# A sliding-window attention and SiLU feed-forward kernel: how the first two attention units are finished, and the order of the work

## The chip, the cores and the metric

The kernel runs on one core of a Trainium2 chip. The core has TensorE (PE, with its weight loads shown apart as PEld), VectorE (DVE), ScalarE (ACT), GpSimd (POOL) and SyncE (SP). In this kernel POOL issues all loads and SP all stores. The metric is the device time in microseconds of one execution.

## The reference

Inputs are `q`, `k`, `v` of shape (8 batches, 8 heads, 576 positions, 64), `w_in` (512 x 2048) and `w_out` (2048 x 512), all in 32-bit floats.

```python
scores = (q @ k.T) / sqrt(64)            # for each batch and head
scores = where(0 <= i - j < 64, scores, -1e9)
attn   = softmax(scores)
x      = (attn @ v), heads side by side   # 4608 tokens x 512
h      = x @ w_in
out    = (h * sigmoid(h)) @ w_out
```

A position sees itself and the 63 before it, so a block of 64 queries needs the keys and values of two blocks of 64.

## The kernel before, in words

**Tiling.** The 72 blocks of 64 positions (9 for each batch) are taken four at a time: 18 units `u`, each 256 tokens wide and all 8 heads deep. The feed-forward part takes 9 tiles `j` of 512 tokens, so tile `j` needs units `2j` and `2j+1`.

**A unit.** Loads bring queries and keys into `nat`. VectorE turns them in 32 x 32 blocks (L322, L332, L335). For the first five units `shift_k` (L311) copies the keys of the block before into place. The score matmuls (L397, L374) fill four PSUM banks, and ScalarE takes the exponential (L403) into `es`. For units 0 and 1 the mask enters the scores as a bias: a matmul of `ident` with `window` (L388). Later units multiply by `mask` on VectorE (L406). The value matmuls (L437, L425) have `es` as the stationary operand and `vv` as the moving one. `vv` has a column of ones beside the 64 values, so each output row carries its own sum in column 64. VectorE inverts 8 sums per row (L442) and multiplies (L445) into `oxs`. For units in `BACK` (0, 1, 2, 3, 5), four PE transposes (L461) and a copy (L464) bring the result into `bridge`, which holds `x` transposed. For the others a DMA transpose on SP does it (L455). Units 0 and 1 do this in two halves `hf`, each with its own PSUM banks.

**Values.** `load_v(b, t)` fills the 128 rows of `vv` at `t` with blocks `t-1` and `t`. For odd `t` it is a load (L345), for even `t` the two halves are copied from the neighbours by `shift_v` (L365, L367). `add_v` takes the list of loads and of copies; `v0` and `v1` hold them for batches 0 and 1.

**Feed-forward.** Tile 0 has its own path. `add_first` issues, for each 128 columns `ft` of `w_in`, four matmuls (L470 from `first_layer`) into one bank and a SiLU (L478). Six `ft` are done first for tokens 0 to 255, then for 256 to 511 (`NF0 = 6`, so that the first half can begin when unit 0 is done), the other ten at full width. `add_plain_second` then runs 64 matmuls of 512 columns, in the order of `f`, and needs `w_out` piece by piece. Later tiles use a form with seven products in place of eight for the second layer, and tiles 6 to 8 for the first layer too (L509).

**What sets the order.** The class `Plan` simulates the engines with costs (`us`), latencies and a model of the DMA queue, and picks at each step, on each free engine, the waiting operation with the lowest `first` (its rank by class). The order it finds is then written out as the program of each engine, so an instruction that waits holds all behind it on its engine. `GO` gives for each unit from 2 on how many feed-forward matmuls must have been issued before its scores may start. `SEQ` is the order of POOL's first loads: `a` to `e` are keys and queries of units 0 to 4, `v` and `y` the next group of value loads of batch 0 and 1, `w` and `o` pieces of `w_in` and `w_out`, `i` the constants. `pick_halves` writes a run of feed-forward matmuls next to value matmuls as pairs of 64 columns each when the run is short against `HALVES`. `UP = 4` puts the scores of unit 1 into banks 4 to 7. A filler matmul on `blank` (L974) keeps PE at work until the first feed-forward matmul.

**Constants.** GpSimd makes `window` and `ident` (L247 to L255) behind the third group of loads. ScalarE copies half of `window` into `window0` (L259), and VectorE makes `mask` (L262, L263). VectorE clears `kt` (L270), the three `vv` (L266, L267) and part of `k2` (L958) at the start.

Of the kernel before, what the change touches and what calls it, by code (L numbers as in the profile page):

```python
# [8 lines left out]
FP32 = mybir.dt.float32  # L9
# [8 lines left out]
class Plan:  # L18
# [7 lines left out]
    def __init__(self, pools, rank):  # L26
        self.rank, self.pools = rank, pools
        self.queues = {}
        self.banks = [[] for _ in range(8)]
        self.count = 0  # L30
        self.halves_cost, self.halves_end, self.halves_not = 0, 0, ()
        self.now = 0.0

    def add(self, cls, us, fn, deps=(), lat=0.2, gate=None, dma=None, pool=None, table=None, rank=None, late=0.0):
        op = dict(us=us, first=self.rank[cls] if rank is None else rank, fn=fn,
                  deps=[d for d in deps if d is not None], lat=lat, gate=gate, dma=dma,
                  pool=pool, table=table, late=late, halve=False, seen=None, n=self.count, until=[], untils=None, bank=None)
        self.count += 1
        self.queues.setdefault(cls, []).append(op)
        return op  # L40
# [99 lines left out]
def kernel(ctx, tc, q, k, v, w_in, w_out, out):  # L140
# [29 lines left out]
    EX = 2  # L170
    LATE = [0, 0, 1, 3, 4, 4, 4, 4]
    scale = 1.0 / float(D) ** 0.5
# [8 lines left out]
    zero = keep.tile([128, 4], FP32, name="zero")  # L181
    spare = keep.tile([128, 4], FP32, name="spare")
# [48 lines left out]
    def pair(op):  # L231
# [3 lines left out]
        {"quad": [(0, 1, 2, 3)], "upper": [(4, 5, 6, 7)], "pp": [(0, 1), (2, 3)], "at": [(0,), (2,)],  # L235
         "mp": [(i,) for i in range(4, 8)], "idle": [(i,) for i in range(4, 8)] + [(0,), (2,)], "all": [(i,) for i in range(8)]},
        rank=dict(one=-9, first=-9, late=5, dma=-1, st=-2, kshift=-16.3, xo=-58.5, turn=11.8, shift=13.7,
                  s=-33.1, exp=-9.0, mask=4.1, pv=27.6, inverse=-8.9, norm=-15.8, ot=-17.4, bridge=-27.4,
                  silu=9.0, moe=99, warm=200, sum=7.1, xsum=-35.5, asum=34.0, plus=-19.9, stage=2.1, wsum=-0.6, piece=-31.8, out=-3.6, prime=-8,
                  turn2=-1.4, turn1=-37.9, shift0=-7.7, shift0b=8.7, shift1=25.9, inverse0=6.3, norm0=1.4, bridge0=16.5,),  # L240
# [5 lines left out]
    def const_ident(_):  # L246
        nc.gpsimd.memset(ident, 0.0)  # L247
        nc.gpsimd.affine_select(out=ident, in_=ident, compare_op=ALU.not_equal, fill=1.0,
                                base=0, channel_multiplier=1, pattern=[[-1, 128]])

    def const_window(_):
        nc.gpsimd.memset(window, 0.0)
        nc.gpsimd.affine_select(out=window, in_=window, compare_op=ALU.is_ge, fill=-32768.0,
                                base=-1, channel_multiplier=1, pattern=[[-1, 64]])
        nc.gpsimd.affine_select(out=window, in_=window, compare_op=ALU.is_ge, fill=-32768.0,  # L255
                                base=64, channel_multiplier=-1, pattern=[[1, 64]])

    def const_window0(_):
        nc.scalar.copy(out=window0[64:128], in_=window[64:128])  # L259

    def const_mask(_):
        nc.vector.tensor_scalar(mask[:, 0], window, 1.0 / 32768.0, 1.0, op0=ALU.mult, op1=ALU.add)  # L262
        nc.vector.tensor_copy(out=mask[:, 1:], in_=mask[:, 0:1].to_broadcast([128, 15, 64]))  # L263
# [9 lines left out]
    c_k = [p.add("one", {"DVE": 0.1}, lambda _, i=i: clear_k(i)) for i in range(2)]  # L273
    c_vv = [p.add("one", {"DVE": 0.4}, lambda _, i=i: clear_vv(i)) for i in range(NVB)]
    c_low = p.add("one", {"DVE": 0.1}, lambda _: nc.vector.memset(window0, -32768.0))
# [8 lines left out]

    def add_consts():
        c_window = p.add("dma", {"POOL": 0.8}, const_window)
        c_ident = p.add("dma", {"POOL": 0.6}, const_ident)
        c_window0 = p.add("prime", {"ACT": 0.25}, const_window0, [c_window, c_low], rank=-9)
        return c_ident, c_window0, p.add("late", {"DVE": 0.8}, const_mask, [c_window])
# [150 lines left out]

    def inverse(op, r, hf):
        nc.vector.reciprocal(out=rcs[r], in_=at_pv(op, hf)[:, :, :, D])  # L442
# [29 lines left out]
    def first_layer(op, bk, j, ft, c, lo, hi):  # L472
        v0 = 4 * j % NBR
        expert_mm(op, bank(bk)[:, lo:hi], w_in_sb[:, c, ft * 128:(ft + 1) * 128],
                  bridge[:, v0 + lo // 128:v0 + hi // 128, c], start=(c == 0), stop=(c == NDC - 1))

    def silu(bk, ft, lo, hi):
        nc.scalar.activation(out=gts[0][:, ft, lo:hi], in_=bank(bk)[:, lo:hi], func=ACTF.Silu)  # L478
# [87 lines left out]
    exps0 = []  # L566
# [31 lines left out]
    def add_v(b, ts, shifts):  # L598
# [4 lines left out]
        for low, a, z in shifts:  # L603
            n = len(range(a, z, 2))
            sh = p.add("shift", {"DVE": 0.1 + 0.2 * n, "ACT": 0.2 + 0.38 * n} if b < 2 else {"DVE": 0.1 + 0.22 * n}, lambda e, low=low, a=a, z=z: shift_v(e, b, low, a, z),
                       [d for t in range(a, z, 2) for d in v_done[b, t - 1 if low else t + 1]],
                       rank=p.rank[("shift0" if a < 4 else "shift0b") if b == 0 else "shift1"] if b < 2 else None)
            for t in range(a, z, 2):
                v_done.setdefault((b, t), []).append(sh)
# [27 lines left out]
    def add_scores_blocks(u):  # L637
        if u < 2:
            bi = p.add("bias", {"PE": 0.95}, lambda _: bias(u), [c_window0, c_ident] + (s_new[0] + kb_done[1][:1] if u else []), pool="upper" if u and UP else "quad", rank=-6)
# [49 lines left out]
    def add_units(u, ready):  # L689
# [8 lines left out]
        for hf in range(2):  # L698
            n = n_unit[0]
# [44 lines left out]
    def add_first(j, pool):  # L744
        jobs = [(ft, 0, TT) for ft in range(NFT)]
        if j == 0:
            jobs = [(ft, 0, HT) for ft in range(NF0)] + [(ft, HT, TT) for ft in range(NF0)] + jobs[NF0:]
        si, bks = {}, {}
        for n, c in [(n, c) for n in range(len(jobs)) for c in range(NDC)]:
            ft, lo, hi = jobs[n]  # L750
            have = [d for i in range((j * TT + lo) // 256, (j * TT + hi) // 256) for d in o_done[i]]
# [3 lines left out]
            op["fn"] = lambda _, op=op, bk=bk, ft=ft, c=c, lo=lo, hi=hi: first_layer(op, bk, j, ft, c, lo, hi)  # L755
            moe.append((op, 1, n == 0 and c == 0, j))
            if c == NDC - 1:
                sl = p.add("silu", {"ACT": 0.18 + (hi - lo) * 0.00082}, lambda _, bk=bk, ft=ft, lo=lo, hi=hi: silu(bk, ft, lo, hi),
                           [op] + g_users[0].get(ft, []) + (exps0 if j == 0 else []), table="silu")
                bk["until"] = [sl]  # L760
                for h in range(lo // HT, hi // HT):
                    si.setdefault((ft, h), []).append(sl)
# [197 lines left out]
    v1 = list(v0)  # L960
    for z in SEQ:
# [4 lines left out]
        elif z == "i":  # L966
            c_ident, c_window0, c_mask = add_consts()
# [11 lines left out]
    c_mask["deps"].append(s_new[0][0])  # L979
# [75 lines left out]
```

## Time and profile before

| what | value |
|---|---|
| median of 3 runs | 281.4 us (281.08 to 281.74) |
| the profiled execution | 282.42 us |
| its span, first to last instruction | 280.6 us |
| mean granted TensorE clock | 0.994 |
| PE busy | 271.8 us (97%) |
| VectorE, ScalarE, GpSimd busy | 203.7, 175.8, 109.3 us |

Times in the rows count from the start of the span. A row of the timeline merges neighbouring instructions of one kind: start, length, engine, line, operation, output and inputs, count, and in brackets the idle time of the engine before it and what ended that. A row of the chain of waits has start, length, and engine with line. A row of the windows has the stretch, its length, then the busy time of PE, PEld, VectorE, ScalarE and GpSimd with instruction counts, the granted clock, and the load of the DMA engines. A row of groups has the shapes and the count, then busy time and mean duration in ns of one, then the idle time before.

### The profile page before, as it was taken

How to read it: one execution, taken by the hardware profiler on the slowest of the kernel's cores; microseconds unless marked ns; L12 is line 12 of the kernel's file. 1: busy time of each engine (PE TensorE's matmuls, PEld its weight loads, DVE VectorE, ACT ScalarE, POOL GpSimd, SP SyncE). 2: the span in 40 equal slices, each digit the busy share in tenths (PEclk: the TensorE clock that was granted, in tenths of full speed). 3: DMA queues.
4: the chain of work that ended last, by engine and by line, in shares of the span. 5: the costliest groups of instructions: out<-in, count | busy, mean ns of one | idle time of the engine just before them, and what ended most of it. 6: DMA issues, size and time to landing. Idle time of an engine off the chain costs nothing.

```text
span 280.6 us, 8735 instructions
## 1 busy us (share of the span) xinstructions
PE 271.8 (97%) x3704; PEld 197.2 (70%) x3704; DVE 203.7 (73%) x380; ACT 175.8 (63%) x272; POOL 109.3 (39%) x163
## 2 busy tenths in 40 slices
PE   8799999999999999899999999999999999999995
PEld 4367445446876488566885488647888888888884
DVE  4682458999868599789698568947587867868641
ACT  2768884976568683857637675665556664565631
POOL 8976776649787599584680000000000000000000
PEclk9979999999999999999999999999999999999999
DMA  9999999999999999999999602540013001101303
GB/s 85 172 197 187 186 185 185 220 220 143 123 217 164 126 146 153 152 177 139 134 165 189 71 2 77 97 96 0 4 37 112 3 32 67 57 0 40 112 20 132
DMA packets 105863, 32.42 MB, mean 116 GB/s; under 512 B 90464, under 2 KB 104800, under 8 KB 105824
## 3 DMA queue, kind: packets, MB, share of 16 engines
q0 software_dynamic: 82336, 19.02, 84.4%
q1 hardware_dynamic: 23488, 12.85, 22.6%
q8 instruction: 29, 0.48, 0.8%
q14 instruction: 10, 0.08, 0.1%
HBM read 38.01 MB, written 9.44 MB: 169 GB/s over the span
## 4 chain that ended last, share of the span: by engine, by line
PE 83%; DMA 8%; issue 3%; DVE 3%; POOL 2%; ACT 1%; DVEq 0%; POOLq 0%; ACTq 0%
PE mp L470 57%; PE la L509 8%; PE la L470 6%; PE mp L509 5%; DMA vv<-in_v_dram 3%; PE at L374 2%; DMA nat<-in_k_dram 2%; PE at L425 2%; DMA nat<-in_q_dram 2%; PE at L437 1%; POOL vv L345 1%; PE at L461 1%; PE mp L974 1%; POOL nat L316 1%; DVE eo L406 1%
## 5 line engine op out<-in xcount | busy, mean ns | idle before, releaser
L470 PE MATMUL mp<-bridge,w_in_sb 128*128 128x512 bf16 (+3 forms) x521 | 86.7, 367 | 0.2 <-ACT gt L478 0.2
L478 ACT ACTIVATE gt<-mp 128x512 bf16<-128x512 f32 (+1 forms) x102 | 56.6, 573 | 22.0 <-PE mp L470 21.2
L470 PEld LDWEIGHTS <-w_in_sb 128*128 128x128 bf16 (+1 forms) x521 | 41.4, 103 | 38.0 <-issue 0.8
L470 PEld LDWEIGHTS <-gs 128*128 128x128 bf16 x512 | 49.4, 98 | 6.0
L403 ACT ACTIVATE eo<-at 128x1024 bf16<-128x1024 f32 x34 | 34.0, 1027 | 14.0 <-PE at L374 12.7
L470 PEld LDWEIGHTS <-gt 128*128 128x128 bf16 (+1 forms) x422 | 34.1, 102 | 9.5 <-issue 0.4
L470 PE MATMUL mp<-ws,gs 128*128 128x256 bf16 x320 | 40.3, 273 | 0.0
L470 PE MATMUL mp<-w_out_sb,gt 128*128 128x256 bf16 (+3 forms) x278 | 38.6, 310 | 0.0
L345 POOL DMA_DIRECT2D vv<-in_v_dram x38 | 33.6, 898 | 3.0 <-DMA w_out_sb<-in_moe_w_out_dram 1.3
L293 POOL DMA_DIRECT2D nat<-in_q_dram x40 | 24.0, 608 | 17.8 <-DMA vv<-in_v_dram 10.0
L406 DVE TENSOR_TENSOR eo<-eo,mask 128x1024 bf16<-128x1024 bf16 x32 | 21.6, 681 | 6.9 <-ACT eo L403 6.7
L293 POOL DMA_DIRECT2D nat<-in_k_dram x40 | 24.2, 617 | 6.1 <-DMA nat<-in_k_dram 3.0
L909 ACT COPY ot<-mp 128x512 f32<-128x512 f32 (+1 forms) x28 | 15.8, 563 | 15.5 <-PE mp L470 14.4
L520 ACT ACTIVATE eo<-vv 128x512 bf16<-128x512 f32 (+1 forms) x18 | 13.9, 773 | 16.2 <-DVE vv L800 16.2
L445 DVE TENSOR_TENSOR eo<-at,rc 128x512 bf16<-128x512 f32 x36 | 22.9, 674 | 0.2
L533 DVE TENSOR_TENSOR gs<-gt 128x1024 bf16<-128x1024 bf16 x24 | 16.3, 686 | 8.5 <-ACT gt L478 8.5
L912 DVE TENSOR_TENSOR ot<-mp,ot 128x512 f32<-128x512 f32 (+1 forms) x21 | 13.8, 658 | 5.7 <-PE mp L470 4.6
L800 DVE TENSOR_TENSOR vv<-mp,vv 128x512 f32<-128x512 f32 x15 | 10.3, 689 | 7.1 <-PE mp L509 7.1
L509 PEld LDWEIGHTS <-w_in_sb 128*128 128x128 bf16 x144 | 14.1, 98 | 1.6
L800 DVE TENSOR_TENSOR vv<-la,vv 128x512 f32<-128x512 f32 x21 | 13.8, 683 | 2.0 <-PE la L509 1.7
L470 PE MATMUL mp<-w_out_sb,gs 128*128 128x256 bf16 x112 | 14.0, 273 | 0.0
L470 PE MATMUL mp<-ws,gt 128*128 128x256 bf16 (+1 forms) x128 | 11.8, 273 | 0.2 <-DVE ot L912 0.2
(121 smaller groups left out, 384.7 us busy)
## 6 DMA issues: line engine op xcount, KB each, us to landing
out_dram<-ot SPq DMA_DIRECT2D x32, 256.0 KB, 3.3
vv<-in_v_dram POOLq DMA_DIRECT2D x38, 128.0 KB, 6.6
nat<-in_k_dram POOLq DMA_DIRECT2D x40, 72.0 KB, 5.8
nat<-in_q_dram POOLq DMA_DIRECT2D x40, 72.0 KB, 5.5
w_in_sb<-in_moe_w_in_dram POOLq DMA_DIRECT2D x8, 256.0 KB, 8.4
w_out_sb<-in_moe_w_out_dram POOLq DMA_DIRECT2D x8, 256.0 KB, 8.1
out_dram<-ot SPq DMA_DIRECT2D x8, 128.0 KB, 1.8
nat<-in_k_dram POOLq DMA_DIRECT2D x3, 256.0 KB, 6.2
```

The lines of the kernel that those rows point to most:

```text
L293: nc.gpsimd.dma_start(out=nats[i].bitcast(BF16)[32 * r:32 * r + 32].rearrange("s (g y) -> s g y", y=128), in_=(q, k)[kk][b, h].rearrange(" ...
L345: nc.gpsimd.dma_start(out=vv[b % NVB][:, t, :, 0:D], in_=v[b, :, 64 * t - 64:64 * t + 64].rearrange("h s d -> s h d"),)
L403: nc.scalar.activation(out=dst, in_=src, func=ACTF.Exp, scale=scale)
L406: nc.vector.tensor_mul(es[w], es[w], mask)
L445: nc.vector.tensor_mul(oxs[o].rearrange("p x c (r d) -> p x (c r) d", r=2), at_pv(op, hf)[:, :, :, 0:D], rcs[r].unsqueeze(3).to_broadcast( ...
L470: nc.tensor.matmul(o[cols], lhsT=w[:, cols], rhs=x, **kw)
L478: nc.scalar.activation(out=gts[0][:, ft, lo:hi], in_=bank(bk)[:, lo:hi], func=ACTF.Silu)
L509: nc.tensor.matmul(bank(bk)[:, HT * f:HT * f + HT], lhsT=w[:, c, 128 * (2 * u + f):128 * (2 * u + f) + 128], rhs=rhs, start=first and f == ...
L520: nc.scalar.activation(out=gt_of(j)[:, f0:f0 + 2, lo:hi], in_=src, func=ACTF.Silu)
L533: (nc.vector.tensor_sub if i else nc.vector.tensor_add)(sums[i][:, f0:f1], x[:, f0:f1], y[:, f0:f1])
L800: d[k] = p.add("plus", {"DVE": 0.69}, lambda _: nc.vector.tensor_add(o, halves(bk), o), [op] + deps)
L909: return p.add("piece", {"ACT": 0.18 + 0.0008 * n}, lambda e: copies[e](out=flat(o), in_=bank(bk)[:, 0:n]), [end] + deps)
```

## The change

- Units 0 and 1 (`TURNED`): the value matmuls swap their operands, so `vv` is stationary (64 columns, without the column of ones) and `es` is moving, and the result lies transposed, as `bridge` wants it. The sums come from matmuls of a 128 x 64 tile of ones with `es` into a second bank, where each sum stands in all 64 rows of its head. VectorE inverts a whole bank of 128 x 512 (`rts`) and multiplies bank by bank into `bridge`. The transposes and copies to `bridge` of these two units go.
- The constants are made on VectorE by `consts` at the start. `window0` and the bias need no other engine. The clearing of `vv[2]` and `kt` and the full `mask` wait for unit 1 (`o_done[1]`).
- Tile 0's half-width jobs take two `ft` in one bank, eight `ft` are done so (`NF0 = 8`), and one SiLU of 128 x 512 serves two `ft`.
- The order: `SEQ`, `GO`, all ranks, `HALVES` and `WHOLE` are new, `NUDGE` moves two single operations, unit 1's scores use banks 0 to 3 (`UP = 0`), and the first value copies of batch 0 are split.

```diff
-    GO = [8, 64, 16, 220, 288, 68, 393, 172, 480, 200, 569, 588, 248, 746, 404, 496]
+    GO = [72, 9, 161, 245, 196, 313, 402, 0, 275, 371, 593, 638, 8, 752, 37, 780]
-    NF0 = 6
-    HALVES = 30
-    WHOLE = []
+    NF0 = 8
+    HALVES = 70
+    WHOLE = [0, 1, 2, 3, 4, 6, 7, 11, 13, 14, 17, 23, 24, 26, 27, 30, 31, 33]
-    SEQ = "a v b i v w w w o w w w y w o w c d o o v y o o e o o y".split()
+    TURNED = (0, 1)
+    SEQ = "a b v w v w w w o w w w w o v c d o o y o y o o o e y".split()
-    UP = 4
+    UP = 0
+    NUDGE = {21: -11.3, 341: 39.7}
...
-    def const_ident(_):
-        nc.gpsimd.memset(ident, 0.0)
-        nc.gpsimd.affine_select(out=ident, in_=ident, compare_op=ALU.not_equal, fill=1.0,
...
+    def consts(_):
+        t = bridge[:, 12:14].rearrange("p v c i -> p (v c i)").bitcast(FP32)
+        col, row, low = t[:, 0:128], t[:, 128:160], t[:, 160:192].bitcast(BF16)
+        nc.vector.memset(col[:, 0:1], 0.0)
+        for w in (1, 2, 4, 8, 16, 32, 64):
+            nc.vector.tensor_scalar_add(col[:, w:2 * w], col[:, 0:w], float(w))
+        nc.vector.transpose(out=row, in_=col[:, 0:32])
+        for r in range(1, 4):
+            nc.vector.tensor_scalar_add(row[32 * r:32 * r + 32, 0:1], row[32 * r:32 * r + 32, 0:1], 32.0 * r)
+        nc.vector.tensor_scalar(col, col, row[:, 0:1], None, op0=ALU.subtract)
+        nc.vector.tensor_scalar(ident, col, 0.0, None, op0=ALU.is_equal)
+        nc.vector.tensor_scalar(low, col[:, 0:64], 0.0, None, op0=ALU.is_lt)
+        nc.vector.scalar_tensor_tensor(out=mask[:, 0], in0=col[:, 0:64], scalar=-64.0, in1=low, op0=ALU.is_ge, op1=ALU.mult)
+        nc.vector.tensor_scalar(window, mask[:, 0], 32768.0, -32768.0, op0=ALU.mult, op1=ALU.add)
+        nc.vector.memset(window0[0:64], -32768.0)
+        nc.vector.tensor_copy(out=window0[64:128], in_=window[64:128])
...
+    def sums_turned(op, u, z):
+        o = bank_at(op["bank"][1]).rearrange("p (c a i) -> p c a i", c=H // 2, a=2)
+        e = es[(2 * u + z) % NE].rearrange("p (a c x) i -> p x a c i", a=2, c=H // 2)
+        for a in range(2):
+            for x in range(2):
+                nc.tensor.matmul(o[64 * x:64 * x + 64, :, a], lhsT=ones, rhs=e[:, x, a], start=(a == 0), stop=(a == 1))
+
+    def values_turned(op, u, z):
+        o = bank_at(op["bank"][0]).rearrange("p (c a i) -> p c a i", c=H // 2, a=2)
+        for a in range(2):
+            b, t = divmod(4 * u + 2 * z + a, NB)
+            for c in range(H // 2):
+                for x in range(2):
+                    nc.tensor.matmul(
+                        o[64 * x:64 * x + 64, c, a], lhsT=vv[b % NVB][:, t, 2 * c + x, 0:D],
+                        rhs=es[(2 * u + z) % NE][:, 8 * a + 2 * c + x], start=(a == 0 and c == 0), stop=(a == 1 and c == H // 2 - 1))
+
+    def inverse_turned(op, z):
+        nc.vector.reciprocal(out=rts[z], in_=bank_at(op["bank"][1]))
+
+    def normal_turned(op, u, z):
+        nc.vector.tensor_mul(bridge_out(u, z).rearrange("p c i -> p (c i)"), bank_at(op["bank"][0]), rts[z])
...
+            if u in TURNED:
+                two = [2 * hf, 2 * hf + 1]
+                sm = p.add("pv", {"PE": 0.3}, None, ready[hf] + [c_ones], pool="pp" if u else "pu", rank=-5.6)
...
-            jobs = [(ft, 0, HT) for ft in range(NF0)] + [(ft, HT, TT) for ft in range(NF0)] + jobs[NF0:]
+            jobs = [(ft, lo, lo + HT) for lo in (0, HT) for ft in range(0, NF0, 2)] + jobs[NF0:]
...
+    v0[0] = ((1, 3), ((0, 0, 2), (1, 2, 4), (0, 2, 4)))
...
-    c_mask["deps"].append(s_new[0][0])
+    for c in [c_mask] + c_vv[2:] + c_k:
+        c["deps"].extend(o_done[1])
+    for sh in shifts_late:
+        sh["deps"].append(exps0[1])
```

More of the change, by code (lines that the diff above doesn't have):

```diff
@@ L181 @@
     zero = keep.tile([128, 4], FP32, name="zero")
+    ones = keep.tile([128, 64], BF16, name="ones")
+    rts = [keep.tile([128, 512], FP32, name=f"rt{i}") for i in range(2)]
     spare = keep.tile([128, 4], FP32, name="spare")
@@ L272 @@
     c_blank = p.add("one", {"DVE": 0.15}, lambda _: nc.vector.memset(blank.bitcast(FP32), 0.0))
[L273 to L275 removed]
+    c_const = p.add("one", {"DVE": 2.0}, consts)
+    c_vv = [p.add("one" if i < 2 else "clear", {"DVE": 0.5}, lambda _, i=i: clear_vv(i)) for i in range(NVB)]
+    c_k = [p.add("clear", {"DVE": 0.1}, lambda _, i=i: clear_k(i)) for i in range(2)]
+    c_mask = p.add("late", {"DVE": 0.7}, const_mask, [c_const])
+    c_ones = p.add("one", {"DVE": 0.1}, lambda _: nc.vector.memset(ones, 1.0))
     c_zero = p.add("one", {"DVE": 0.1}, lambda _: nc.vector.memset(zero, 0.0))
@@ L283, in load_wide @@
         )
[L285 to L289, printed above, removed]
     def load_rows(i, b, h, kk):
```

79 lines of the change are left out of this document (44 added, 35 removed).

## The prediction

> **What bounds the kernel now.** I read the page first, then PE's busy time by stretches of the span.
>
> ```profile
> span 280.6 us, 8735 instructions
> PE 271.8 (97%) x3704; PEld 197.2 (70%) x3704; DVE 203.7 (73%) x380; ACT 175.8 (63%) x272; POOL 109.3 (39%) x163
> ...
> 10.70:15.20 4.50, 2.16 (x85) 1.19 (x82) 3.98 (x8) 3.29 (x5) 4.38 (x7) 1.00 1.87 180
> 15.20:19.30 4.10, 4.10 (x74) 2.61 (x66) 3.39 (x8) 3.55 (x6) 3.19 (x4) 0.58 1.38 198
> 19.30:33.70 14.40, 14.40 (x114) 9.07 (x111) 4.98 (x11) 11.38 (x24) 9.91 (x13) 1.00 1.69 186
> 33.70:52.00 18.30, 18.30 (x369) 10.00 (x368) 13.61 (x27) 12.77 (x20) 12.94 (x18) 1.00 1.60 190
> ...
> 191.50:276.70 85.20, 85.20 (x783) 76.37 (x781) 60.80 (x99) 47.06 (x80) 0.00 (x0) 1.00 0.14 46
> ```
>
> PE is full from 19.3 us to the end. So a change pays if it starts the feed-forward part earlier, shortens PE's work, or removes one of PE's few waits. The start is read from the timeline and from the chain of waits.
>
> ```profile
> 5.65 0.71 DVE L322 STREAM_TRANSPOSE kt<-nat 128x512 f32<-128x512 f32 x1 [2.08 <-DMA nat<-in_k_dram]
> 7.09 0.72 DVE L322 STREAM_TRANSPOSE qt<-nat 128x512 f32<-128x512 f32 x1 [0.21 <-DMA nat<-in_q_dram]
> 8.05 0.29 DVE L365 COPY vv<-vv 64x512 bf16<-64x512 bf16 x1 [0.23 <-DMA vv<-in_v_dram]
> 9.61 0.33 DVE L365 COPY vv<-vv 64x512 bf16<-64x512 bf16 x1 [1.27 <-DMA vv<-in_v_dram]
> 11.06 0.71 DVE L322 STREAM_TRANSPOSE gs<-nat 128x512 f32<-128x512 f32 x1 [1.12 <-DMA nat<-in_k_dram]
> 14.58 0.21 DVE L442 RECIPROCAL rc<-at 128x8 f32<-128x8 f32 x1
> 19.29 1.25 PE L470 MATMUL mp<-bridge,w_in_sb 128*64 128x256 bf16 x20
> 21.59 12.29 PE L470 MATMUL mp<-bridge,w_in_sb 128*128 128x256 bf16 x72
> 33.71 0.59 PE L470 MATMUL mp<-w_out_sb,gt 128*128 128x512 bf16 x2
> ```
>
> The loads land one after the other, 1.45 us apart for keys and queries and 2.5 us for two of values. Unit 0 is ready to be inverted at 12.3 us but waits until 14.58, because VectorE is turning unit 1 (11.06 to 14.55). Then come inverse, multiply, transpose and copy for two halves, and the first feed-forward matmul starts at 19.29. From there tile 0's first layer runs without a hole until 33.7.
>
> **The new start, loads.** Two rows of the DMA view give issue to landing of the fourth and the eighth piece of `w_in`:
>
> ```profile
> 12.72 0.83 POOL L351 DMA_DIRECT2D w_in_sb<-in_moe_w_in_dram  x1
> w_in_sb<-in_moe_w_in_dram POOLq DMA_DIRECT2D x1, 256.0 KB, 8.1
> ...
> 19.78 0.77 POOL L351 DMA_DIRECT2D w_in_sb<-in_moe_w_in_dram  x1 [0.58 <-DMA w_out_sb<-in_moe_w_out_dram]
> w_in_sb<-in_moe_w_in_dram POOLq DMA_DIRECT2D x1, 256.0 KB, 9.5
> ```
>
> They land at 12.72 + 8.1 = 20.8 and 19.78 + 9.5 = 29.3. Between them lie four pieces of weights and two of values, 8.5 us, so about 1.35 a piece of weights if a piece of values takes 0.75 to 1.25. In the new order the fourth piece has one piece of `w_out` less ahead of it: 20.8 - 1.35 = 19.5. The eighth has one piece of `w_out` and two of values less: about 26.5. Counting back from 19.5, pieces 3, 2 and 1 land near 18.1, 16.8 and 13.3. Unit 1's keys and queries now follow unit 0's (8.5 and 10.0), and the first values come at 12.5 instead of 9.6. POOL loses its constants, but they cost no landing: the load behind them, issued at 8.04, still queued behind others for 5 us.
>
> **The new start, VectorE.** These rows price it:
>
> ```profile
> L445 DVE TENSOR_TENSOR eo<-at,rc 128x512 bf16<-128x512 f32 x36 | 22.9, 674 | 0.2
> L912 DVE TENSOR_TENSOR ot<-mp,ot 128x512 f32<-128x512 f32 x19 | 13.0, 682 | 4.9 <-PE mp L470 3.8 <-ACT eo L403 0.7
> L912 DVE TENSOR_TENSOR ot<-mp,ot 128x256 f32<-128x256 f32 x2 | 0.8, 424 | 0.8 <-PE mp L470 0.8
> L442 DVE RECIPROCAL rc<-at 128x8 f32<-128x8 f32 x36 | 6.7, 197 | 3.4 <-PE at L425 2.3 <-PE at L437 0.2
> L262 DVE TENSOR_SCALAR mask<-window 128x64 bf16<-128x64 bf16 x1 | 0.4, 380 | 0.0
> L276 DVE MEMSET zero<- 128x4 f32 x1 | 0.1, 62 | 0.0
> ```
>
> - Constants: 17 small instructions, between 0.06 and 0.38 each by the last two rows, 1.0 to 6.5 us. I take 0.2 each, 3.4 us, since both kinds are among them. With two clearings of `vv` and the rest, VectorE is free at about 6.0 instead of 5.65. The cover is the wait for the first keys. At the upper bound the first turn slips to 9.0, and the value loads, which wait for the clearing, slip by 1.1 us with all behind them: 1.1 us lost.
> - Reciprocal of a whole bank: not in this trace. The 256- and 512-wide rows give 1.0 ns an element and 0.17 fixed. Lower bound 0.17 + 512 ns = 0.68. If what the 128x8 inverse has above the fixed part (0.207 - 0.168 for 8) were all by element, 5 ns each, it is 2.7 us. I take 0.7: the bank's shape and path are those of L445 and L912, and the small inverse reads single columns 65 apart, which explains its rest as well. The Trainium skill (VectorE: DVE Perf Modes, "First, the fixed hardware budget") says that reciprocal runs iterated divide steps with a repeat count of 8; taken as eight cycles an element, my estimate from that page would be 4.4 us, and no run here has shown it.
> - The sum: from 8.5 us on VectorE has two turns (1.4), two of the key copies (1.1), four reciprocals (2.8), four multiplies (2.7), six value copies (2.3): 10.3 us, so unit 1 is in `bridge` at 18.8 or later, and unit 0 about 14.5. Values of unit 1 land near 16.2, then copy, value matmul and two multiplies end by 19 as well.
>
> **The new start, PE.** Clearing, mask and transposes are off its path. What PE adds (sums and turned values, 20 matmuls in place of 16 for each half) is bounded by the value matmuls that go, 0.5 us a half from below, and 0.9 with four 256-wide ones at 0.11 each. It lies in holes, because tile 0's first half now waits for `w_in`. The 32 matmuls of 256 columns per half (0.109 each: 64 of them in 7.0) come in four groups of 0.87 us with pieces 1.35 apart, so the first half ends 0.87 after the fourth piece: 20.4. The granted clock speaks for a little more:
>
> ```profile
> 12.00:13.00 1.00, 0.26 (x16) 0.14 (x10) 0.97 (x3) 0.97 (x2) 1.00 (x3) 1.00 2.33 175
> 13.00:14.00 1.00, 0.11 (x2) 0.10 (x2) 0.94 (x3) 0.98 (x2) 1.00 (x2) 1.00 1.46 186
> 16.00:17.00 1.00, 1.00 (x4) 0.49 (x4) 0.94 (x3) 1.00 (x3) 0.93 (x2) 0.50 1.45 201
> 18.00:19.00 1.00, 1.00 (x27) 0.80 (x26) 0.51 (x2) 0.90 (x2) 0.49 (x1) 0.50 1.40 199
> ```
>
> PE's idle time before 15 us brought the clock to half from 16 to 19. Now it hits feed-forward work: 0 to 0.6 us more, and I take 0.3. So the second half starts at 20.7 (unit 1 is in by then), runs 3.5 us, and eight full `ft` follow at 4 x 0.214 = 0.855 each, 6.85 us, with the eighth piece there in time: 31.05 against 33.7. **Gain 2.65 us** (3.3 at best).
>
> **After 31 us.** The bytes loaded until 49 us are the same, and the last pieces of `w_out` come earlier, so tile 0's second layer should hold its 18.3 us less what moved. PE's other waits are these:
>
> ```profile
> 55.67 4.41 PEld L470 LDWEIGHTS <-w_in_sb 128*128 128x128 bf16 x21 [0.37 <-issue]
> 117.97 0.54 PE L425 MATMUL at<-vv,eo 128*64 128x65 bf16 x22 [1.20 <-issue]
> 144.27 1.94 PE L470 MATMUL mp<-ws,gt 128*64 128x256 bf16 x32 [0.24 <-DVE ot L912]
> ...
> 42.68 0.51 PE at L437 x32
> 63.39 0.63 PE at L437 x32
> ```
>
> With two smaller ones they sum to 2.1 us. The gates of late units move by up to 34 matmuls (unit 13 from 588 to 638, of which 8 are tile 0's longer list), which can shift each wait either way. Bounds: 2.1 gained, or the 2.65 given back where loads, which do not move, set the time. I take 0.5 gained, since the later gates put scores where the loads are surely there. `HALVES` and `WHOLE` choose at which value matmuls PE changes its tiling; the last two rows show 0.12 us for one side. At most five units can gain or lose that: 0.6 either way, taken as 0.
>
> **Sum.** 282.42 for the profiled execution (280.6 span and 1.8 around it) less 2.65 and 0.5 is 279.27. That execution was 1.0 above the median of 281.4, so the median becomes **278.2**.
>
> **Rivals.**
> 1. *More*: the clock holds (0.3), all waits go (1.6 beyond mine) and halving pays 0.6: near 275.7. For it: every wait is short and has its own cause. Against it: a fixed order cannot remove all.
> 2. *Given back*: the gain turns into waits of units 7 to 13. For it: the chain of waits leaves PE between 122 and 147 us.
>
> ```profile
> 125.00 9.72 DMA vv<-in_v_dram
> 135.01 5.56 DMA nat<-in_q_dram
> ```
>
> There loads, not PE, set the time of unit 13, though PE idled only 0.4 us. If its place in PE's order stays, PE waits the 2.65 us instead: 281.4. Against it: its gate moves back.
> 3. *Slower by a misplaced unit*: unit 2's scores may now follow the 72nd matmul of tile 0, at about 25.9 us. Its queries land near 31.3 (26.5 for the eighth piece, then a piece of `w_out` 1.35, half a piece of values 0.6, keys and queries 2.9) and are ready at 32.2. If the planner's DMA model runs ahead and puts them there, PE, which takes its program in order, stands for 6.3 us: 278.2 + 6.3 = 284.5. It is slower than before from a wait of 3.2 us. Against it: before, the gate was 8 and the scores still came after 90 matmuls, at 34.2, once loaded.
> 4. *Slow reciprocals*: at 2.7 us each VectorE's sum grows by 8.0, unit 1 is in at 26.8, the first layer ends at 37.2, 3.5 later than before: 284.4 with the 0.5 kept. Slower from about 1.9 us each, where unit 1 comes in after 23.8. By the skill's figure it would be about 291.
> 5. *It does not do what it says*: the constants at their upper bound leave 1.1 us less, 279.3, within the forecast's own range.
>
> **How the numbers follow.** Forecast and rival 5, 276.8 to 280.5: 0.60. More: 0.12. Given back: 0.11, of which 0.07 within 0.2%. Misplaced: 0.10. Slow reciprocals: 0.05. Unnamed: 0.02. About 0.2%, 0.6 us, is what a measurement here can tell from no change. Faster 0.76, same 0.07, slower 0.17. The range 275.2 to 282.0 leaves the two slow rivals out; the likeliest case's own is 276.8 to 280.5.
>
> **What would show it.** Right: feed-forward starts near 14.5 to 15.5 us with holes until 20 to 21, each ended by a piece of `w_in`; the first 512-wide matmul on `w_out` near 31; whole-bank reciprocals of 0.7 us; no ACT or PE work for transposes of units 0 and 1. Wrong: reciprocals of over 1.9 us, VectorE still busy with constants after 7 us, a wait of PE's scores of unit 2, or waits after 50 us that sum to more than 4 us.

## The result, and the profile after

The changed kernel takes 289.51 us in the median (289.47 to 290.75, four runs), the kernel before 281.24 in the same runs (279.96 to 281.74): a ratio of 1.031 with a 95% interval of [1.027, 1.036]. Forecast were 278.2 us and a range of 275.2 to 282.0, so the sign was wrong. The profiled execution took 290.75 us, 8.3 more than that of before.

The page of the changed kernel and then its stretches come first, with the columns as in the prediction. The stretches end at unit 0's scores, at the first feed-forward matmul, at the start of tile 0's second layer, at tile 1, at tile 6 and at the end.

```profile
span 289.0 us, 8803 instructions
PE 273.7 (95%) x3739; PEld 198.5 (69%) x3739; DVE 219.9 (76%) x400; ACT 171.3 (59%) x258; POOL 108.6 (38%) x158
```

```profile
0.00:11.44 11.44, 8.14 (x29) 3.67 (x30) 9.36 (x32) 2.52 (x3) 10.41 (x17) 0.85 1.32 118
11.44:22.86 11.42, 7.03 (x195) 4.17 (x194) 10.49 (x11) 7.82 (x10) 6.67 (x10) 1.00 1.58 192
22.86:43.67 20.81, 17.22 (x132) 10.93 (x132) 11.95 (x15) 9.24 (x16) 14.89 (x20) 0.84 1.64 187
43.67:62.01 18.34, 17.94 (x280) 9.10 (x279) 14.36 (x31) 10.84 (x16) 13.14 (x20) 1.00 1.65 172
62.01:200.68 138.67, 138.47 (x2331) 94.84 (x2331) 112.40 (x216) 94.60 (x136) 63.48 (x94) 1.00 1.24 126
200.68:285.60 84.92, 84.87 (x778) 75.83 (x775) 61.35 (x99) 45.90 (x79) 0.00 (x0) 1.00 0.14 48
```

Tile 0's second layer starts at 43.67 us and not at 33.7 as before, nor at the forecast 31.05. Ten microseconds are lost before it, and 1.6 of them come back later: between tile 1 and tile 6 PE idles 0.2 us (138.67 less 138.47). The answering row of before, with the same columns, is

```profile
51.96:192.24 140.28, 138.44 (x2208) 93.39 (x2207) 112.47 (x214) 94.19 (x135) 69.40 (x104) 1.00 1.48 136
```

with 1.8 us idle. Where the ten are lost shows in VectorE's timeline of the changed kernel:

```profile
1.12 2.03 DVE L256 TENSOR_SCALAR bridge<-bridge 128x1 f32<-128x1 f32 x7
...
5.81 0.18 DVE L266 COPY window<-window 64x64 bf16<-64x64 bf16 x1
...
7.91 0.71 DVE L324 STREAM_TRANSPOSE kt<-nat 128x512 f32<-128x512 f32 x1
...
13.71 3.36 DVE L461 RECIPROCAL rt<-mp 128x512 f32<-128x512 f32 x1 [0.61 <-PE mp L448]
...
18.66 3.35 DVE L461 RECIPROCAL rt<-mp 128x512 f32<-128x512 f32 x1
22.11 0.69 DVE L464 TENSOR_TENSOR bridge<-mp,rt 128x512 bf16<-128x512 f32 x1
22.84 0.56 DVE L369 COPY vv<-vv 64x1024 bf16<-64x1024 bf16 x1
23.42 3.36 DVE L461 RECIPROCAL rt<-at 128x512 f32<-128x512 f32 x1
...
29.12 3.36 DVE L461 RECIPROCAL rt<-at 128x512 f32<-128x512 f32 x1 [0.92 <-PE at L456]
32.51 0.69 DVE L464 TENSOR_TENSOR bridge<-at,rt 128x512 bf16<-128x512 f32 x1
```

The reader is to see that a reciprocal of a bank takes 3.36 us where a multiply of the same 128 x 512 takes 0.69. The four of them fill 13.4 of the 19.5 us from 13.71 to the end of the last multiply. PE stands for them, by its timeline:

```profile
6.04 1.02 PE L390 MATMUL at<-window,ident 128*128 128x512 bf16 x4 [2.18 <-DVE window L266]
...
22.86 0.93 PE L495 MATMUL mp<-bridge,w_in_sb 128*128 128x256 bf16 x7 [2.51 <-DVE bridge L464]
26.83 0.64 PE L456 MATMUL at<-eo,vv 128*64 128x64 bf16 x16 [3.05 <-DVE rt L461]
...
33.26 10.57 PE L495 MATMUL mp<-bridge,w_in_sb 128*128 128x256 bf16 x64 [0.54 <-DVE bridge L464]
```

The wait at 26.83 holds feed-forward matmuls too, since they stand behind unit 1's value matmuls in PE's order. The first 46 us of the chain of waits say the same by shares: `DVE rt L461` has 29.1% of them.

### The profile page after: what moved, and what is told of

Read it like the earlier page. It is cut to its first block, busy times and chain, and to the rows that moved or that the text cites. A ratio compares the mean times of both kernels' runs of the same rounds, so it can differ in the third digit from the quotient of the medians.

```text
span 289.0 us, 8803 instructions
## 1 busy us (share of the span) xinstructions
PE 273.7 (95%) x3739; PEld 198.5 (69%) x3739; DVE 219.9 (76%) x400; ACT 171.3 (59%) x258; POOL 108.6 (38%) x158
## 4 chain that ended last, share of the span: by engine, by line
PE 88%; DVE 7%; ACT 2%; issue 1%; DVEq 0%
PE mp L495 60%; PE la L536 8%; PE la L495 6%; PE mp L536 5%; DVE rt L461 5%; PE at L376 3%; PE at L427 2%; PE mp L1021 2%; PE at L399 1%; PE at L439 1%; ACT eo L405 1%; DVE bridge L256 1%; PE at L486 1%; DVE bridge L464 1%; ACT L505 0%
## 5 line engine op out<-in xcount | busy, mean ns | idle before, releaser
L495 PE MATMUL mp<-bridge,w_in_sb 128*128 128x512 bf16 (+2 forms) x532 | 88.2, 370 | 3.6 <-DVE bridge L464 3.1
L505 ACT ACTIVATE gt<-mp 128x512 bf16<-128x512 f32 x96 | 55.4, 599 | 30.0 <-PE mp L495 29.6
L495 PEld LDWEIGHTS <-w_in_sb 128*128 128x128 bf16 (+1 forms) x532 | 43.0, 104 | 40.9 <-issue 3.7
L495 PEld LDWEIGHTS <-gs 128*128 128x128 bf16 (+1 forms) x534 | 49.7, 99 | 5.8
L405 ACT ACTIVATE eo<-at 128x1024 bf16<-128x1024 f32 x36 | 35.8, 1025 | 15.8 <-PE at L376 9.2
L495 PE MATMUL mp<-ws,gs 128*128 128x256 bf16 (+1 forms) x342 | 39.9, 273 | 0.0
L495 PE MATMUL mp<-w_out_sb,gt 128*128 128x256 bf16 (+3 forms) x285 | 38.0, 299 | 0.0
L347 POOL DMA_DIRECT2D vv<-in_v_dram x38 | 34.2, 920 | 6.6 <-PE mp L495 2.8
L470 DVE TENSOR_TENSOR eo<-at,rc 128x512 bf16<-128x512 f32 x32 | 20.3, 677 | 0.3 <-DVE rc L467 0.2
```

What stands on the lines that cost most here:

```text
L347: nc.gpsimd.dma_start(out=vv[b % NVB][:, t, :, 0:D], in_=v[b, :, 64 * t - 64:64 * t + 64].rearrange("h s d -> s h d"),)
L405: nc.scalar.activation(out=dst, in_=src, func=ACTF.Exp, scale=scale)
L470: nc.vector.tensor_mul(oxs[o].rearrange("p x c (r d) -> p x (c r) d", r=2), at_pv(op, hf)[:, :, :, 0:D], rcs[r].unsqueeze(3).to_broadcast( ...
L495: nc.tensor.matmul(o[cols], lhsT=w[:, cols], rhs=x, **kw)
L505: nc.scalar.activation(out=gts[0][:, ft:ft + n, lo:hi], in_=bank(bk).rearrange("p (f t) -> p f t", f=n), func=ACTF.Silu)
```

## Experiments

All medians stand against the kernel before, run on the same chip in the same session (280.95 to 281.87 us over the sessions). Two runs from different sessions are therefore compared only to within some 0.9 us.

**Copies for reciprocals.** The order, all buffers and all other instructions stay.

```diff
-        nc.vector.reciprocal(out=rts[z], in_=bank_at(op["bank"][1]))
+        nc.vector.tensor_copy(out=rts[z], in_=bank_at(op["bank"][1]))
```

> The changed kernel with the four reciprocals of a whole bank (3.36 us each in its trace) replaced by copies of the same 128x512 bank; units 0 and 1 are then multiplied by their sums instead of divided. Theory A (the reciprocals made the loss): VectorE saves 4 x 2.65 = 10.6 us, the first 512-wide matmul on w_out moves from 43.7 to between 31 and 34 us, the time is 277 to 280. Theory B (constants, new load order and the mode of the start made it): first layer still ends after 40, time over 285.

Measured: 282.55 us, ratio 1.002 [0.998, 1.007]. The copies take 0.69 us each, and the second layer starts at 34.55. By the medians, 7.0 of the 8.3 us lost hang on the reciprocals; by the ratios to the kernel before, 1.031 against 1.002, nearly all of them do. But with reciprocals at just the price that the prediction gave them the kernel is still not faster than before, and the time meets neither expectation.

**Reciprocal in two halves.** Is the 3.36 us a fixed cost, or does it go by elements?

```diff
-        nc.vector.reciprocal(out=rts[z], in_=bank_at(op["bank"][1]))
+        for a in range(2):
+            nc.vector.reciprocal(out=rts[z][:, 256 * a:256 * a + 256], in_=bank_at(op["bank"][1])[:, 256 * a:256 * a + 256])
```

> The changed kernel with each reciprocal of 128x512 cut into two of 128x256. If the time goes by element, one takes 0.17 + 256 x 6.23 ns = 1.77 us and the pair 3.5; if 3.36 is a fixed price of the operation, each takes about 3.3. Whole time by element: within 1 us of the changed kernel's 289.5; with the fixed price: 300 or more.

Two groups of this kernel and then two of the changed kernel (busy time, mean ns of one):

```profile
L462 DVE RECIPROCAL rt<-at 128x256 f32<-128x256 f32 x4 | 6.7, 1726 | 0.9 <-PE at L456 0.9
L462 DVE RECIPROCAL rt<-mp 128x256 f32<-128x256 f32 x4 | 6.7, 1724 | 1.5 <-PE mp L448 1.5
```

```profile
L461 DVE RECIPROCAL rt<-at 128x512 f32<-128x512 f32 x2 | 6.7, 3358 | 1.0 <-PE at L456 0.9
...
L467 DVE RECIPROCAL rc<-at 128x8 f32<-128x8 f32 x32 | 5.5, 190 | 7.6 <-PE at L427 5.5 <-PE at L439 1.5
```

(3358 - 1725) / 256 is 6.4 ns an element, with 0.09 us fixed. The one run took 290.95 us, 1.4 above the median of the changed kernel, where 1 us was expected at most. By these two figures 8 elements would take 0.14 us, and the small inverse takes 0.19. The cost goes by elements, as the prediction's upper bound read it out of that small inverse.

**Constants.** First on the kernel before, alone: `consts` on VectorE, with the planner told 5.0 us for it, and GpSimd's constants gone.

```diff
-    c_low = p.add("one", {"DVE": 0.1}, lambda _: nc.vector.memset(window0, -32768.0))
+    c_const = p.add("one", {"DVE": 5.0}, consts)
...
-    SEQ = "a v b i v w w w o w w w y w o w c d o o v y o o e o o y".split()
+    SEQ = "a v b v w w w o w w w y w o w c d o o v y o o e o o y".split()
```

> The kernel before with one part of the change: window, ident, window0 and the first mask column made on VectorE at the start (5.0 us in the planner's cost), GpSimd's constants and ScalarE's copy removed. The changed kernel's trace shows these instructions from 1.0 to 6.0 us and the first key turn at 7.9 in place of 5.65. Theory A: unit 0 starts 2 to 2.5 us later, partly hidden behind the loads of unit 1 (landing at 11.0), time 281 to 283.5. Rival (they are the larger half of the loss): over 285. Other rival (GpSimd's freed 1.5 us pays): under 280.5.

Measured: 280.84, ratio 0.998 [0.995, 1.001]. No difference can be told, and the time lies between the ranges expected. This kernel was planned anew and GpSimd lost its constants in it, so the run tells both together. Then on the changed kernel, where they are taken off VectorE: three memsets in their place, and the identity on GpSimd behind the third load, once with copies for the reciprocals and once with the reciprocals.

```diff
     def consts(_):
...
+        nc.vector.memset(window, 0.0)
+        nc.vector.memset(window0, 0.0)
+        nc.vector.memset(mask[:, 0], 1.0)
```

> The run with copies in place of the reciprocals, and also the constants' chain on VectorE replaced by three memsets (ident by GpSimd behind the third load); the planned order stays word for word. It leaves out the division and the masks of units 0 to 4. In the run with copies alone the scores of unit 0 came at 12.4 us and the second layer of tile 0 began at 34.55. Theory A (what is still missing of the forecast is the constants, 5.0 us where the planner reckons 2.0): scores of unit 0 by 9.7, second layer at 31 to 33, time 278 to 280.5. Rival (the loads of w_in or the clock set that start anyway): second layer at 34 to 35, time 281.5 to 283.

> The whole-bank reciprocals stay, the constants are memsets (the band of the mask in units 0 to 4 and its bias are left out), the order is that of the changed kernel. If the reciprocals set the time on top of a start that is given back, unit 0's scores start near 8.4 us, the second layer of tile 0 near 41 us (43.7 less the 2.5 that the constants took), and the total is 287.0 to 288.6: dearer by about 5 than the same kernel with copies in place of reciprocals (282.5). If the constants were a good part of the loss, it is below 285. If the fixed order gives back any start, it is 289 or more.

Measured: 282.52, ratio 1.004 [1.000, 1.008], with copies; 290.14, ratio 1.031 [1.027, 1.036], with reciprocals. The four kernels make a square:

| | constants as in the change | memsets |
|---|---|---|
| reciprocals | 289.51 | 290.14 |
| copies | 282.55 | 282.52 |

Reciprocals cost 7.0 in the one column and 7.6 in the other. The constants cost nothing that can be told in either row, though they do hold the start: with copies and memsets the first feed-forward matmul comes at 15.44 us and not at 19.38, and the second layer at 32.06 and not at 34.55. A part of this is the execution and not the constants: in two kernels further below, which start with the same instructions, the first feed-forward matmul came at 17.12 and 17.94 us and the second layer at 32.34 and 33.11. The time expected for the reciprocals with memsets, 287.0 to 288.6, was missed by 1.5. The start that it counted on (unit 0's scores near 8.4) came at 10.61, and the second layer at 42.85, only 0.8 us before that of the changed kernel. The last section has the rows of this start.

These 2.5 us of an earlier start are gone by tile 6, which begins at 193.15 us with copies and memsets, at 192.40 with copies alone and at 192.24 before. The first of these executions took 0.8 us more than its kernel's median, the last 1.0. The chain of waits from 40 to 200 us, by its shares: first the changed kernel, then the one with copies, then the one with copies and memsets.

```profile
by line: PE mp L495 83.4%; PE at L376 5.2%; PE at L427 4.0%; PE at L439 1.3%; PE at L399 1.2%; PE at L486 1.0%; ACT L505 0.8%; ACT kt L313 0.8%; issue 0.7%; ACT eo L405 0.7%; ACT gt L505 0.4%; ACT ot L902 0.4%; ACT bridge L489 0.4%
```

```profile
by line: PE mp L495 40.3%; DMA vv<-in_v_dram 10.5%; POOL nat L295 8.9%; DMA nat<-in_k_dram 8.2%; DMA nat<-in_q_dram 8.1%; issue 8.0%; POOL vv L347 3.9%; PE at L376 2.3%; PE at L427 2.3%; PE la L536 2.3%; DVE eo L470 0.9%; POOL nat L288 0.8%
```

```profile
by line: PE mp L493 38.6%; POOL nat L288 13.3%; DMA nat<-in_k_dram 10.9%; DMA nat<-in_q_dram 9.2%; issue 7.3%; POOL vv L345 6.6%; DMA vv<-in_v_dram 6.3%; PE at L374 2.3%; PE at L425 2.3%; PE la L534 2.2%; DVE eo L468 0.4%; POOL nat L313 0.4
...
108.75 6.22 DMA nat<-in_k_dram
...
118.51 6.65 DMA nat<-in_q_dram
125.40 0.58 issue
126.79 0.69 DVE eo L468
127.97 6.49 PE mp L493 x38
```

With the late start of the changed kernel PE sets the time from 40 us on. In the two kernels with copies the chain runs through loads and their issue on GpSimd until 125 us, and only then through PE alone. The last wait of PE there ends on VectorE (`eo` at 126.79), which stood behind a turn that waited for queries. So there are two candidates for what takes the gain: the loads, or VectorE. The next three runs are to tell them apart.

**Half of the values' bytes, or a short mask.** Both on the kernel with copies and memsets, in the same order with the same instructions.

```diff
+        n = H // 2 if b > 2 else H
         nc.gpsimd.dma_start(
-            out=vv[b % NVB][:, t, :, 0:D],
-            in_=v[b, :, 64 * t - 64:64 * t + 64].rearrange("h s d -> s h d"),
+            out=vv[b % NVB][:, t, 0:n, 0:D],
+            in_=v[b, 0:n, 64 * t - 64:64 * t + 64].rearrange("h s d -> s h d"),
```

> The kernel with copies for reciprocals and memsets for constants, whose value loads of batches 3 to 7 bring only 4 of 8 heads (half of the values of these batches are left out; every instruction stays). If loads pin the middle of the kernel, TensorE's waits between tile 1 and tile 6 fall from 3.9 to under 2 us, tile 6 starts at 190 to 191.5 instead of 193.15, the chain of waits no longer runs through DMA rows from 40 to 125 us, and the time is 279.3 to 281.2. If VectorE pins it, nothing moves: 282.5 within 0.6, tile 6 near 193.

```diff
-        nc.vector.tensor_mul(es[w], es[w], mask)
+        nc.vector.tensor_mul(es[w][:, 0:1], es[w][:, 0:1], mask[:, 0:1])
```

> The same kernel with copies and memsets; the mask multiplications of units 2 to 17 touch 64 of 1024 columns (most of the masking is left out), which frees VectorE by some 0.6 us each, about 20 us in all. If loads pin the middle, nothing moves: 282.5 within 0.6, tile 6 near 193, and the chain still runs through DMA rows. If VectorE pins it, the waits fall under 2 us, tile 6 starts at 190 to 191.5, and the time is 279.3 to 281.2.

Measured: 280.06, ratio 0.996 [0.993, 0.998], with half of the values; 281.61, ratio 1.001 [0.998, 1.005], with the short mask. The same row of the chain, first for half of the values, then for the short mask:

```profile
by line: PE mp L494 71.1%; DMA vv<-in_v_dram 7.4%; PE at L375 5.1%; PE at L426 4.3%; PE la L535 2.7%; DVE gs L559 1.9%; issue 1.1%; POOL nat L281 0.8%; DVE kt L332 0.8%; DVE qt L332 0.7%; PE at L438 0.6%; PE at L485 0.6%; DVE ws L564 0.6%; 
```

```profile
by line: PE mp L493 52.6%; DMA nat<-in_q_dram 7.9%; DMA nat<-in_k_dram 6.5%; issue 5.9%; DMA vv<-in_v_dram 5.9%; POOL nat L288 5.1%; POOL vv L345 5.0%; PE at L374 2.3%; PE at L425 2.3%; PE la L534 2.2%; PE at L437 1.2%; ACT kt L306 0.8%; PE
```

Fewer bytes bring tile 6 to 190.31 us and take 2.5 us off, as was expected if the loads pin the middle. GpSimd still issues as many loads, so it is their bytes and not their number. Fewer bytes also bring the executions closer together: from 280.57 to 284.76 us with copies and memsets, from 279.60 to 281.28 with half of the values.

The short mask takes 15.6 us of work off VectorE, by the groups with the whole mask and with the short one:

```profile
L406 DVE TENSOR_TENSOR eo<-eo,mask 128x1024 bf16<-128x1024 bf16 x32 | 21.1, 673 | 4.8 <-ACT eo L403 4.5
L406 DVE TENSOR_TENSOR eo<-eo,mask 128x64 bf16<-128x64 bf16 x32 | 5.5, 178 | 8.6 <-ACT eo L403 8.4
```

Tile 6 still begins at 193.45 us, with the chain in the loads. But the execution in the profile is the second slowest of twelve, 2.0 us above their median. That median is 0.9 us lower than with the whole mask, which lies inside the intervals, and it meets neither expectation. So the loads pin the middle, and that VectorE plays a small part in it is not excluded.

**The control.** The same cut of bytes on the kernel before.

> The control to e12_half_values: the kernel before with the same cut (value loads of batches 3 to 7 bring 4 of 8 heads, half of the values of these batches left out). If the early start is worth its 1.4 to 2 us once loads no longer pin the middle, this kernel stays 1 us or more above e12_half_values' 280.06: 281.0 or more, since its own waits between tile 1 and tile 6 (2.2 us) come only in part from loads, and it still starts the second layer of tile 0 at 33.7. If the cut of the loads alone made e12's gain, it comes down as far: 280.1 or less, tile 6 near 190.

Measured: 280.31, ratio 0.997 [0.995, 1.000], tile 6 at 189.91. That lies between the two expectations and near the second. The new order with copies and memsets is 0.25 us from the kernel before once bytes are taken from the loads of both, which can't be told from nothing. In this execution the kernel before started its second layer at 32.27 us, the new order with half of the values at 32.34. So the new order started no earlier here, and what an earlier start is worth with fewer bytes to load stays open. In the execution that the prediction was made from the second layer came at 33.71, with the same instructions up to there: so a part of the gain that was forecast was the lateness of one execution.

**Shorter fillers.** Copies, constants as in the change, fillers of 128 columns in place of 384, to see whether unit 0's scores wait behind fillers.

```diff
-        nc.tensor.matmul(bank(op)[:, 0:384], lhsT=blank[:, 0:128], rhs=blank, start=True, stop=True)
+        nc.tensor.matmul(bank(op)[:, 0:128], lhsT=blank[:, 0:128], rhs=blank[:, 0:128], start=True, stop=True)
```

> The run with copies in place of the reciprocals, and the filler matmuls cut from 384 to 128 columns. 17 of them, placed by the planner, took 4.8 us ahead of unit 0's scores. If they hold the scores: scores at 10.2 to 10.8 in place of 12.4, time 280 to 282. If the keys and queries hold them: scores still after 12, time as with copies alone, 282 to 283.

Measured: 281.40, ratio 1.001 [0.998, 1.004]: 1.15 us less than with long fillers, with overlapping intervals. Unit 0's scores came at 10.21 us and not at 12.44, so the long fillers had held them; what they wait for now is VectorE's turn of the queries. The execution with this row took 2.9 us more than the median.

```profile
10.21 1.04 PE L399 MATMUL at<-qt,kt 32*128 32x64 bf16 x64 [0.46 <-DVE qt L324]
```

**The old finish, and a true price.** One run sets `TURNED = ()`, so that units 0 and 1 are finished as before under the new ranks; another tells the planner 3.36 us for the reciprocal.

```diff
-                rc = p.add("inverse", {"DVE": 0.69}, lambda _, sm=sm, hf=hf: inverse_turned(sm, hf), [sm] + rt_users.get(hf, []),
+                rc = p.add("inverse", {"DVE": 3.36}, lambda _, sm=sm, hf=hf: inverse_turned(sm, hf), [sm] + rt_users.get(hf, []),
```

> The changed kernel with units 0 and 1 finished in the old way (TURNED empty: values with a column of ones, inverse of 128x8, multiply, PE transpose, copy to bridge); constants, load order, paired d_ff tiles and all ranks stay new. Theory A: no instruction over 1.3 us on VectorE in the start, first layer ends at 32 to 36, time 279 to 283. Theory B: no better than 285.

> The changed kernel with one number of the planner changed: 3.36 in place of 0.69 us for the reciprocals, so that the order is made for what they take. Theory A: the work itself is the loss, the time stays within 285 to 290. Rival (the loss is the wrong order that the wrong cost led to): the time falls to 283 or less.

Measured: 299.58, ratio 1.064 [1.057, 1.070], and 300.33, ratio 1.067 [1.062, 1.071]. Both change the order that the planner writes, and both are slower than the changed kernel by some 10 us. The first falls where its theory B had it, the second meets neither expectation. ScalarE's groups of the old finish, then its stretch of tile 0's second layer:

```profile
L405 ACT ACT_TABLE_LOAD x8 | 10.3, 1283 | 1.0 <-PE at L399 0.5 <-PE at L376 0.5
L505 ACT ACT_TABLE_LOAD x8 | 10.3, 1283 | 2.3 <-PE mp L495 2.2
```

```profile
40.74:64.27 23.53, 19.70 (x142) 9.85 (x144) 16.64 (x31) 10.26 (x15) 16.23 (x25) 0.78 1.58 169
```

Each of the two runs has 18 table loads of 1.28 us where the kernel before and the changed one have 12, and in the first PE idles 3.8 us in tile 0's second layer at a clock of 0.78. These two runs were to isolate the finish and don't, so they don't speak for theory B either: ranks, `GO` and `NUDGE` hold for one set of costs, and a new plan from them mixes in another order. Only runs that keep the written order tell a single cost.

**A small division.** The sums as 128 x 8 (one column of `ones` as moving operand), a small inverse, eight matmuls with `ident` that spread it over a bank, a copy on ScalarE. Once planned anew, once with the written order kept, and once kept with the constants on GpSimd behind the third load and short fillers.

```diff
-        nc.vector.reciprocal(out=rts[z], in_=bank_at(op["bank"][1]))
+        nc.vector.reciprocal(out=rss[z], in_=bank_at(op["bank"][1])[:, 0:H])
+        nc.vector.tensor_copy(out=rbs[z], in_=rss[z].unsqueeze(2).to_broadcast([128, H, 64]))
+        spread(op, z)
+        nc.scalar.copy(out=rts[z], in_=bank_at(op["bank"][1]))
```

> The changed kernel with the sums taken as 128x8 (matmuls with one column of ones), inverted at that size (0.2 us), spread to 64 columns by a VectorE copy, and turned and broadcast into the bank by eight matmuls with ident, then copied to rt by ScalarE. Same result, no large reciprocal. Theory A: start within 1.5 us of the run with copies in place of reciprocals, time 278 to 281.5. Theory B: over 285.

> The changed kernel with a true division that needs no large reciprocal: sums as 128x8, inverse at that size, spread by VectorE, turned and broadcast into the bank by eight matmuls with ident, copied out by ScalarE. Unlike the earlier run of this idea (297.9 us) it adds no operation to the plan, so the order of the changed kernel stays. Theory A (that run lost by its new order, not by the work): 281.5 to 285. Rival (the added matmuls and copies are the loss): 290 or more.

> The same small division with the kept order, and the constants back on GpSimd, behind the third load, and fillers of 128 columns. Right result. Theory A: first feed-forward matmul by 17, second layer of tile 0 at 31.5 to 33.5, time 278 to 281, below both kernels. Rival: over 282.

Measured: 297.90, ratio 1.057 [1.049, 1.064]; 286.24, ratio 1.016 [1.010, 1.022]; 289.27, ratio 1.031 [1.024, 1.038]. The first, planned anew, has 18 table loads as well. The second lies between its two expectations, the third far above the 278 to 281 hoped for. VectorE's groups with the order kept:

```profile
L470 DVE CAST rb<-rs 128x512 bf16<-128x512 f32 x4 | 1.7, 427 | 0.1
L469 DVE RECIPROCAL rs<-at 128x8 f32<-128x8 f32 x2 | 0.4, 208 | 0.2 <-PE at L464 0.2
```

0.64 us in place of 3.36, and 3.3 us won back against the changed kernel. The rest is a chain: inverse, cast, spreading on PE, copy on ScalarE, multiply, 2.5 to 3.8 us for each half by the timeline, with three hand-overs, and PE waits in order. In the third version the wait has a second price, in these stretches:

```profile
9.00:20.00 11.00, 7.57 (x234) 5.07 (x231) 6.45 (x14) 5.87 (x8) 8.86 (x13) 0.84 1.74 177
20.00:30.00 10.00, 9.22 (x106) 6.20 (x107) 4.95 (x14) 5.39 (x10) 5.74 (x8) 0.50 1.54 192
```

PE idled 3.4 of the 11 us up to 20 us, and the granted clock was 0.50 for the ten after it, which are tile 0's first layer. Its first feed-forward matmul comes at 20.69 us, earlier than in the changed kernel, its second layer at 41.23. Which of its edits left PE idle is not separated.

No version here that does the whole work beats the kernel before by more than can be told.

## Why the prediction was wrong

- **Reciprocal of a whole bank: the step that failed.** The prediction put 0.7 us on it, since "the bank's shape and path are those of L445 and L912", and explained the rest of the small inverse by its column stride. Measured: 3.36, above even the upper bound of 2.7, which came from the difference of two small durations, 0.207 and 0.168, too coarse to be drawn out to 512 elements. The 0.7 came from rows of another operation at the right shape; the row of the right operation at another shape was the better guide. The column stride explains nothing: in the small division the inverse of eight neighbouring columns takes 0.208 us, no less than the 0.190 of the one with the stride. The Trainium skill (VectorE: DVE Perf Modes, "First, the fixed hardware budget") spoke for iterated steps, and the estimate from it, 4.4 us, is nearer to the measured 3.36 than 0.7 is. 6.4 ns an element is six times the 1.0 ns of the 256- and 512-wide rows.
- **Slow reciprocals (rival 4)** is what happened, with the place right and the size short. Its formula gives 284.4 + 4 x 0.66 = 287.0 for 3.36 us, and 289.5 came. The difference is where VectorE's sum begins: not at 8.5 us but at 13.71, because the first inverse waits for scores, exponential and sums. From there the prediction's rows, with 3.36 for the reciprocals, add up to 18.4 us; 19.5 passed, since VectorE waited twice for PE. So unit 1 was in `bridge` at 33.2, 3.8 us later than by the formula. The 10.4 us from there to the second layer are those of the prediction, and later 1.6 us came back in place of 0.5.
- **Constants.** 3.4 us by the prediction, 5.0 measured (1.01 to 6.00), inside the bounds. They are 19 instructions; the prediction counted 17. The cover named, the wait for the first keys, was too short, and PE waited 2.18 us for `window`, which the prediction had not seen. No cost to the end can be told in three comparisons, one of them planned anew.
- **Loads** came as forecast: the first four pieces of `w_in` at 13.06, 16.09, 18.46 and 19.68 us against 13.3, 16.8, 18.1 and 19.5, the eighth at 26.31 against 26.5.
- **The new start.** With copies and memsets the first feed-forward matmul came inside 14.5 to 15.5 and the second layer at 32.06 against 31.05. The 1.0 is the fourth piece of `w_in`, 20.73 against 19.68 in the changed kernel. GpSimd made the identity first and issued the group of three that it belongs to at 9.84 us and not at 9.05; that it landed later for this is not shown. So the working of the start can hold where VectorE's prices do. But it was luck that this execution showed it: the two other kernels with copies and the same start had the first feed-forward matmul at 17.12 and 17.94 us. And the gain of 2.65 was counted against an execution whose second layer started 1.4 later than in another with the same start.
- **After 31 us** is not settled. 0.5 us was to come from later waits. The changed kernel gained 1.6 there, but with a start 10 us late, for which the term was not made. With copies the stretch from tile 1 to tile 6 took 139.51 us in the profile against 140.28 before, so 0.8 were gained. With copies and memsets, the earliest start, it took 142.74: there the start was given back to loads, as rival 2 had it, though earlier than in units 7 to 13, with the chain in the loads from 40 us on. Rival 2 gave 281.4; the kernels with copies and all bytes measured 281.40 to 282.55. The slow reciprocals lie on top.
- **Misplaced unit 2** did not come: tile 0's second layer takes 18.34 us in the changed kernel, 18.25 before. What the halving is worth no run isolated.

## What to carry to other kernels

Price an operation that the trace lacks by the row of the same operation first, whatever its shape, and only then by the shape: between an upper bound of 2.7 and a lower one of 0.7 stood the sign of the forecast. Before an early start is booked as a gain, follow the chain of waits behind it: where it runs through loads at any place, as it did in the kernel before from 125 us on, the gain may end there. Test one cost in a written order by swapping the instruction alone; a planner that is run again answers another question.

## What the runs showed of the hardware

The start is not the same in two executions of the same instructions. The kernels with the short mask and with copies and memsets have one program up to unit 0's scores, and these are the timeline and then one stretch of the first, and the same of the second:

```profile
4.64 1.89 PE L388 MATMUL at<-window,ident 128*128 128x512 bf16 x4 [0.78 <-POOL ident L258]
6.32 4.74 PE L1019 MATMUL mp<-blank 128*128 128x384 bf16 x17
```

```profile
6.00:7.00 1.00, 1.00 (x5) 0.39 (x4) 0.76 (x2) 0.62 (x1) 1.00 (x2) 1.00 1.79 177
```

```profile
4.66 1.04 PE L388 MATMUL at<-window,ident 128*128 128x512 bf16 x4 [0.79 <-POOL ident L258]
5.54 2.93 PE L1019 MATMUL mp<-blank 128*128 128x384 bf16 x17
```

```profile
6.00:7.00 1.00, 1.00 (x9) 0.59 (x7) 0.84 (x2) 0.54 (x1) 1.00 (x2) 1.00 1.75 173
```

The same 17 fillers took 4.74 and 2.93 us, both at a granted clock shown as 1.00, so unit 0's scores came at 10.99 and at 8.39. The two other kernels with this start lie between, with 3.90 and 4.34 us and scores at 10.18 and 10.61. A start read from a single profile is therefore uncertain by 2.6 us. In the changed kernel the same fillers also run five in a microsecond, and there the granted clock is shown as 0.50:

```profile
9.00:10.00 1.00, 1.00 (x5) 0.46 (x4) 0.97 (x2) 0.86 (x2) 1.00 (x3) 0.50 2.09 168
```

A clock at half that its record leaves out would explain the slow starts. That is not shown, and the cause stays open.
